# First expert, second half: seven block products, token sums on GpSimd, one scaling for both halves

## Chip, core and metric

One core of a Trainium2 chip runs the whole program in one launch. The metric is the device time of an execution in microseconds (us). The kernel before takes 1096.43 us (median of 3 runs, 1096.05 to 1096.6). The engines have one instruction queue each and run it in order: TensorE (PE in the profile; its weight loads are PEld), VectorE (DVE), ScalarE (ACT), GpSimd (POOL), SyncE (SP), which issues the DMAs here.

## The reference

```python
def _attn_ref(q, k, v, f):                  # (2, 8, 576, 64) each, f the forget gates
    scores = scale * q @ k.T + (cum[:, None] - cum[None, :])   # cum = cumsum(log f), causal
    return softmax(scores) @ v

def _moe_ref(x, w_gate, w1, w2):            # x: 1152 tokens x 512, 8 experts, 1024 hidden features
    P = np.exp(logits - logits.max())       # logits = x @ w_gate
    for _ in range(8):
        P /= P.sum(1, keepdims=True) + 1e-09
        P /= P.sum(0, keepdims=True) + 1e-09
        P *= N / E
    for e in range(E):
        h = np.maximum(x @ w1[e], 0.0)
        out += P[:, e:e + 1] * (h @ w2[e])
    return out

def _moe2_ref(x, w_in, w_out):              # 512 -> 2048 -> 512
    h = x @ w_in
    return (h * np.tanh(softplus(h))) @ w_out
```

Three layers one behind the other: attention, eight experts that all see every token with a weight P per token and expert, and a last feed-forward layer. The change lies at the start of the experts.

## The kernel before, in words

Every fp32 value that goes through TensorE is held as two parts, high and low ("h" and "l": ScalarE writes the high part as a rounded copy, VectorE or GpSimd the low part as the remainder, value minus high part). A product of two such values is three matmuls: high by high, high by low, low by high.

An expert's 1024 hidden features are two halves of 512; halves are numbered 0 to 15 over the eight experts. Tokens go in three chunks of 384 (`CH`). One plain unit (`l1`, line 816 on) is one feature block of 128 for one chunk: 4 input blocks by 3 matmuls of 384 columns, into one PSUM bank. `relu_split` (L832, L833) makes the two hidden parts from it. The second layer (`l2_tile`, L855) multiplies hidden blocks of 128 tokens by w2, 512 columns wide, three matmuls for each feature block.

From half 2 on the first layer isn't plain. `pair(half, n, tasks)` computes two feature blocks by two by a Strassen-like scheme with 7 block products in place of 8. It needs sums of blocks of w1 (S1 to S4: `new_sum`, `s_sum`, `s_split`) and sums of blocks of tokens (T1 to T3: `t_whole`, `t_diff`, `t_split`; `t_first` replaces one block of x by its sum with others). `t_whole` adds high and low parts back together, in two instructions of 576 columns; `t_diff` and `t_split` are 1152 columns wide. The tokens of a block fall in two sets of 288 columns, so there are two pairs for a half (n = 0 and 1), each with 14 products of 6 matmuls of 288 columns (`product`, L1263). Out of the PSUM banks ScalarE copies partial products ("snap", L1292), VectorE adds others to them ("c", L1297), and `relu_split` ends a block. The order within a pair is the list `plan`: products 1, 2, 1, 6, 2, 6, 7, 5, 7, 4, 5, 4, 3, 3 (each twice, for two feature blocks). `tasks` are small jobs that are put between these products: evictions, the splits of w2 (`w2_tasks`), pieces of a decoding of later weights.

The token sums serve all 15 later halves, as x doesn't change, so they are made once. In the kernel before this happens during the first expert, which is computed the plain way:

- Half 0, chunks 0 and 1, run as filler work between attention's steps, and are evicted to `acc[0..5]`.
- Then a loop over 8 feature blocks does chunk 2 of both halves: 8 plain units, and behind each the second layer of the one before, all into the three banks `psa`. Between them the background work goes: the splits of half 1's w1 and w2 (`bg`), the token sums (`tbg`, on VectorE), and the steps of the balancing iteration for P (`sinkhorn`, one part at each `step_side`; its column sums are small matmuls against a matrix `ones`).
- Then 8 plain units for half 1, chunks 0 and 1, with the rest of `tbg`, and `scale_first` for chunk 2 (ScalarE scales `psa` by P into `acc[6..8]`).
- Then `second(1, c)` for c = 0 and 1: the second layer of half 1, with the splits of half 2 and the scaling of `acc[0..5]` between. Its evictions add P times the bank to `acc`.

`second` takes `slots`, a list of jobs, one entry after each nine matmuls. Loads of weights are DMAs on SyncE (`Weights.load`, L61), each issued as soon as the buffer that it fills is split. The tile framework sets all waits; the order of instructions on each engine is the order of the code.

Of the kernel before, what the change touches and what calls it, by code (L numbers as in the profile page):

```python
# [83 lines left out]
def attention_moe_kernel(  # L84
# [734 lines left out]
    def l1(half, ft_, c, pool, tag="h"):  # L819
        w = wts.slots[half]  # L820
        fs = slice(ft_ * 128, (ft_ + 1) * 128)
        ph = pool.tile([128, 512], F32, tag=tag, name="ph")[:, :CH]
        for kk in range(KD):
            for n, (wn, x) in enumerate((("w1h", xh), ("w1h", xl), ("w1l", xh))):
                nc.tensor.matmul(  # L825
                    out=ph, lhsT=w[wn][kk][:, fs], rhs=x[c][:, kk],
                    start=(kk == 0 and n == 0), stop=(kk == KD - 1 and n == 2),
                )
        return ph
# [30 lines left out]
    def sinkhorn():  # L860
# [9 lines left out]
        nc.tensor.matmul(out=mb[:, :1], lhsT=ones[:1, :], rhs=m2, start=True, stop=True)  # L870
# [3 lines left out]
        for it in range(ITERS):  # L874
# [9 lines left out]
            nc.tensor.matmul(out=cp, lhsT=ones, rhs=cs, start=True, stop=True)  # L884
# [6 lines left out]
            )  # L891

# [156 lines left out]
    def new_sum(half, i, in0, in1, op):  # L1049
        t = sum_pool[0].tile([128, 2, 256], F32, tag="tmp", name="sum")  # L1050
        nc.vector.tensor_tensor(out=t, in0=in0, in1=in1, op=op)
# [12 lines left out]
    def s_split(half, i):  # L1064
# [3 lines left out]
        nc.vector.tensor_tensor(out=lo, in0=t, in1=f(hi), op=ALU.subtract)  # L1068
# [31 lines left out]
    hctx = ExitStack()  # L1100
    actx = ExitStack()
    hp = actx.enter_context(tc.tile_pool(name="hp", bufs=2))
    ttmp = actx.enter_context(tc.tile_pool(name="ttmp", bufs=1))
    ones = ttmp.tile([128, 128], F32, name="ones")
    nc.gpsimd.memset(ones, 1.0)
    ps_h = hctx.enter_context(tc.tile_pool(name="ps_h", bufs=2, space=PSUM))
    ps_a = hctx.enter_context(tc.tile_pool(name="ps_a", bufs=3, space=PSUM))

    def new_h():
        return (  # L1110
            hp.tile([128, CH], FR, tag="hh", name="hh"),
            hp.tile([128, CH], FR, tag="hlo", name="hlo"),
        )

    wts.load(1, 2, stage_b)

    def plain_split(n):
        wts.split(1, n // 2, n % 2)
        if n == 3:
            for p in (0, 1):  # L1120
                wts.raw.pop((1, p))
                wts.load(2, p, stage)

    bg = [lambda n=n: plain_split(n) for n in range(4)] + w2_tasks(1)


# [14 lines left out]
    def t_whole(r, side, k):  # L1141
        for n in range(2):
            nc.vector.tensor_tensor(
# [7 lines left out]
    def t_split(i, r):  # L1151
        hi, lo = (t[:, TW * (i - 1):TW * i] for t in (th, tl))
        nc.scalar.copy(out=hi, in_=r)
        nc.vector.tensor_tensor(out=lo, in0=r, in1=f(hi), op=ALU.subtract)

    def t_first(n):
# [3 lines left out]
        nc.vector.tensor_tensor(out=lo, in0=r, in1=f(hi), op=ALU.subtract)  # L1160

    tbg = [
        lambda: t_whole(r11, 0, 0),
        lambda: t_whole(r12, 1, 0),
        lambda: t_diff(r11, r12, r11),
        lambda: t_whole(r22, 1, 2),
        lambda: t_diff(r12, r22, r12),
        lambda: t_split(2, r12),
        lambda: t_diff(r22, r22, r11),
        lambda: t_split(1, r22),  # L1170
        lambda: t_whole(r12, 0, 2),
        lambda: t_diff(r12, r12, r22),
        lambda: t_split(3, r12),
    ]
# [3 lines left out]
    NF = F // 128
    step_side()
    for g in range(NF):  # L1180
        half, gg = g // 4, g % 4
        ph = l1(half, gg, 2, ps_h)
        h = new_h()
        relu_split(ph, *h)
        step_side()
        for _ in range(2):
            if bg:
                bg.pop(0)()
        for _ in range((0, 0, 0, 0, 1, 2, 2, 2)[g]):
            tbg.pop(0)()  # L1190
# [4 lines left out]
    firsts = [lambda j=j: scale_first(6 + j, psa[j]) for j in range(3)]
    firsts += [lambda t=t: scale_first(t, acc[t]) for t in range(6)]
    for g in range(4):
        for c in range(2):
            last_l1 = (g, c) == (3, 1)
            relu_split(l1(1, g, c, *((ps_m, "m") if last_l1 else (ps_h, "h"))), *hidden(g, c))  # L1200
            if g == 0 and c == 0:
                for j in range(3):
                    l2_tile(*prev[:2], psa[j], j, prev[2], prev[3] == 0, prev[3] == NF - 1)
            if side:
                if (g, c) != (0, 1):
                    step_side()
            elif len(firsts) > 6:
                firsts.pop(0)()
            if tbg and g:
                tbg.pop(0)()  # L1210
    assert not (bg or tbg or side)
    assert len(firsts) <= 6
    for n in range(2):
        t_first(n)
    actx.close()
    hctx.close()


    dec = mctx.enter_context(tc.tile_pool(name="dec", bufs=2))
    tmp = mctx.enter_context(tc.tile_pool(name="tmp", bufs=4))  # L1220
    sum_pool.append(tmp)
    ps_b = ctx.enter_context(tc.tile_pool(name="ps_b", bufs=1, space=PSUM))
    banks = [ps_b.tile([128, 512], F32, name=f"bank{i}") for i in range(7)]

    def next_bank():
        banks.append(banks.pop(0))
# [655 lines left out]
```

## Time and profile before

| | |
|---|---|
| median of 3 runs | 1096.43 us (1096.05 to 1096.6) |
| the profiled execution | 1096.1 us, span 1094.3 us |
| TensorE busy, of the span | 1085.1 us, 99% |
| VectorE | 842.0 us, 77% |
| ScalarE | 542.6 us, 50% |
| GpSimd | 75.5 us, 7%, none of it after 157.7 us |
| granted TensorE clock | 1.000 |
| chain that ended last | TensorE 91%, VectorE 4%, DMA 2%, ScalarE 1% |

The span is from the first to the last instruction; the execution's own time has 1.8 us more around it. Busy matmul times overlap each other, as a matmul starts before the one ahead of it has ended; the pace is read from the start times. The experts begin at 162.65 us, and the second expert's first product starts at 231.93.

### The profile page before, as it was taken

How to read it: one execution, taken by the hardware profiler on the slowest of the kernel's cores; microseconds unless marked ns; L12 is line 12 of the kernel's file. 1: busy time of each engine (PE TensorE's matmuls, PEld its weight loads, DVE VectorE, ACT ScalarE, POOL GpSimd, SP SyncE). 2: the span in 40 equal slices, each digit the busy share in tenths (PEclk: the TensorE clock that was granted, in tenths of full speed). 3: DMA queues.
4: the chain of work that ended last, by engine and by line, in shares of the span. 5: the costliest groups of instructions: out<-in, count | busy, mean ns of one | idle time of the engine just before them, and what ended most of it. 6: DMA issues, size and time to landing. Idle time of an engine off the chain costs nothing.

```text
span 1094.3 us, 18378 instructions
## 1 busy us (share of the span) xinstructions
PE 1085.1 (99%) x6838; PEld 964.9 (88%) x6838; DVE 842.0 (77%) x1891; ACT 542.6 (50%) x1287; POOL 75.5 (7%) x124
## 2 busy tenths in 40 slices
PE   9999999999999999999999999999999999999998
PEld 8787779998989899898888989899898989888997
DVE  7856647878787887977888796887877559778994
ACT  7756532444426243342624435252442448877872
POOL 6644410000000000000000000000000000000000
PEclk9999999999999999999999999999999999999999
DMA  6534202023242424425343342534323341261402
GB/s 147 147 84 113 65 21 78 1 97 124 87 137 68 144 86 146 136 78 155 97 153 96 118 150 92 154 87 145 116 89 95 115 156 48 68 202 51 172 1 87
DMA packets 103805, 114.98 MB, mean 105 GB/s; under 512 B 35236, under 2 KB 63860, under 8 KB 103716
## 3 DMA queue, kind: packets, MB, share of 16 engines
q1 hardware_dynamic: 103716, 113.81, 33.8%
q8 instruction: 54, 0.88, 0.3%
q14 instruction: 35, 0.29, 0.1%
HBM read 82.24 MB, written 27.07 MB: 100 GB/s over the span
## 4 chain that ended last, share of the span: by engine, by line
PE 91%; DVE 4%; DMA 2%; ACT 1%; issue 1%; SPq 0%; POOL 0%; DVEq 0%; ACTq 0%
PE bank L855 31%; PE bank L1263 27%; PE bank L1735 9%; PE bank L1645 4%; PE ph L825 3%; PE x L567 2%; PE spare L1645 2%; PE bank L1574 2%; PE pa L855 2%; PE pa L640 2%; PE ph L621 1%; DMA w_in_b<-hb 1%; PE sp L467 1%; PE pt L531 1%; PE pt L360 1%; PE sp L415 1%
## 5 line engine op out<-in xcount | busy, mean ns | idle before, releaser
L855 PE MATMUL bank<-w2h,big 128*128 128x512 f32 x924 | 300.2, 394 | 0.0
L855 PEld LDWEIGHTS bank<-w2h,big 128*128 128x128 f32 x924 | 173.8, 188 | 38.7 <-DVE hid_b L833 0.2
L855 PE MATMUL bank<-w2l,big 128*128 128x512 f32 x528 | 207.5, 393 | 0.0
L1292 ACT COPY snap<-bank 128x288 f32<-128x288 f32 x168 | 66.9, 398 | 170.3 <-PE bank L1263 169.9
L832 ACT ACTIVATE big<-c 128x288 fp32r<-128x288 f32 x168 | 75.2, 447 | 86.6 <-DVE c L1297 82.6
L855 PEld LDWEIGHTS bank<-w2l,big 128*128 128x128 f32 x528 | 99.3, 188 | 20.9
L833 DVE SCALAR_TENSOR_TENSOR big<-c,big 128x288 fp32r<-128x288 f32 x140 | 64.1, 458 | 57.1 <-ACT big L832 54.5
L1028 DVE SCALAR_TENSOR_TENSOR acc<-bank,P,acc 128x512 f32<-128x512 f32 x132 | 92.5, 747 | 19.3 <-PE bank L855 19.3
L1263 PE MATMUL bank<-tt,ss 128*128 128x288 f32 x672 | 103.5, 295 | 0.4 <-ACT snap L1292 0.4
L1263 PE MATMUL bank<-xh,ss 128*128 128x288 f32 x448 | 103.4, 296 | 0.2 <-DVE c L1297 0.2
L1263 PEld LDWEIGHTS bank<-tt,ss 128*128 128x128 f32 x672 | 93.9, 188 | 0.8 <-ACT snap L1292 0.8
L1297 DVE TENSOR_TENSOR c<-bank,snap 128x288 f32<-128x288 f32 x168 | 76.0, 453 | 19.7 <-PE bank L1263 19.4
L1263 PEld LDWEIGHTS bank<-xh,ss 128*128 128x128 f32 x448 | 76.7, 188 | 0.4 <-DVE c L1297 0.4
L1008 ACT CAST hb<-da 128x512 fp32r<-128x512 f32 x38 | 23.7, 623 | 107.3 <-DVE da L986 95.9
L1263 PE MATMUL bank<-xl,ss 128*128 128x288 f32 x224 | 66.5, 297 | 0.0
L1263 PE MATMUL bank<-xh,w1l 128*128 128x288 f32 x224 | 66.2, 295 | 0.0
L1263 PE MATMUL bank<-xl,w1h 128*128 128x288 f32 x224 | 66.1, 295 | 0.0
L1263 PE MATMUL bank<-xh,w1h 128*128 128x288 f32 x224 | 66.1, 295 | 0.0
L75 DVE TENSOR_TENSOR w2l<-stg,w2h 128x512 fp32r<-128x512 f32 x60 | 41.3, 690 | 14.0 <-ACT w2h L74 13.7
L855 PE MATMUL bank<-w2h,hid_b 128*128 128x512 f32 x132 | 51.6, 391 | 0.0
L511 POOL TENSOR_SCALAR p<-p,rs 128x256 f32<-128x256 f32 (+5 forms) x72 | 42.3, 598 | 65.1 <-DVE rs L507 42.9
L1263 PE MATMUL bank<-tt,w1h 128*128 128x288 f32 x224 | 46.4, 295 | 0.0
(314 smaller groups left out, 2460.7 us busy)
## 6 DMA issues: line engine op xcount, KB each, us to landing
stg<-in_moe_w_dram SPq DMA_DIRECT2D x64, 512.0 KB
wb<-w_in_b SPq DMA_DIRECT2D x42, 256.0 KB
raw<-in_moe_w_in_dram SPq DMA_DIRECT2D x16, 512.0 KB
raw<-in_moe_w_out_dram SPq DMA_DIRECT2D x16, 512.0 KB
w_in_b<-hb SPq DMA_DIRECT2D x18, 256.0 KB
w_out_h<-hb SPq DMA_DIRECT2D x16, 256.0 KB
w_out_l<-da SPq DMA_DIRECT2D x16, 256.0 KB
w_in_f<-da SPq DMA_DIRECT2D x12, 256.0 KB
```

What stands on the lines that cost most here:

```text
L75: (lo_engine or nc.vector).tensor_tensor(out=lo, in0=raw, in1=f(hi), op=ALU.subtract)
L511: nc.gpsimd.tensor_scalar(out=p[:n, a, :nk], in0=p[:n, a, :nk], scalar1=r[:n, a:a + 1], scalar2=1.0, op0=ALU.mult, op1=ALU.mult,)
L825: nc.tensor.matmul(out=ph, lhsT=w[wn][kk][:, fs], rhs=x[c][:, kk], start=(kk == 0 and n == 0), stop=(kk == KD - 1 and n == 2),)
L832: nc.scalar.activation(out=hh, in_=ph, func=AF.Relu)
L833: nc.vector.scalar_tensor_tensor(out=hl, in0=ph, scalar=0.0, in1=f(hh), op0=ALU.max, op1=ALU.subtract)
L855: nc.tensor.matmul(out=pa, lhsT=a_[:, ts_], rhs=w[wn][ft_], start=(first and n == 0), stop=(last and n == 2),)
L1028: nc.vector.scalar_tensor_tensor(out=acc[t], in0=pa, scalar=P[:, t, e:e + 1], in1=acc[t], op0=ALU.mult, op1=ALU.add)
L1263: nc.tensor.matmul(out=by_chunk(out_) if len(v_.shape) == 3 else out_, lhsT=u, rhs=v_, start=first and m == 0, stop=m == 5, skip_group_che ...
L1292: nc.scalar.copy(out=t, in_=bank["x", g])
L1297: nc.vector.tensor_tensor(out=t, in0=bank[of, g], in1=snap[with_, g], op=ALU.add)
L1645: nc.tensor.matmul(out=out_, lhsT=a_(kk, pa), rhs=b_(kk, pb), start=first and q == 0, stop=q == 5, skip_group_check=True,)
L1735: nc.tensor.matmul(out=bk[b][:, cs], lhsT=a_[:, ts_], rhs=w[wn][i][:, cs], start=i == 0 and q == 0, stop=i == 3 and q == 2,)
```

## The change

Half 1 goes through `pair` like the halves behind it. What the plain units hid before has to be ready sooner: the loop at the start shrinks to the four units of half 0, chunk 2, and the sums of w1's blocks for half 1 are needed too. So work moves to GpSimd: `t_whole`, the sums of w1's blocks, most of the low parts of half 1's weights and sums, and the low parts of T3 and of one half of `t_first`. Expert 0's halves are added without P (`evict` for e = 0 is an addition; `settle` copies `psa` to `acc[6..8]`), and all nine parts are scaled during the second expert. The scratch pool `tmp` and the seven PSUM banks are opened ahead of the loop; the decoding's first transfers come behind the first pair. `ones` is replaced by a broadcast column, and `sinkhorn` stops twice in an iteration instead of once.

```diff
@@ sinkhorn
-            nc.tensor.matmul(out=cp, lhsT=ones, rhs=cs, start=True, stop=True)
+            nc.tensor.matmul(out=cp, lhsT=one_row.to_broadcast([128, 128]), rhs=cs, start=True, stop=True)
...
+            yield
@@ evict
         t = c * 3 + j
+        if e == 0:
+            nc.vector.tensor_tensor(out=acc[t], in0=pa, in1=acc[t], op=ALU.add)
+            return
@@ new_sum
-        nc.vector.tensor_tensor(out=t, in0=in0, in1=in1, op=op)
+        (nc.vector if half > 1 else nc.gpsimd).tensor_tensor(out=t, in0=in0, in1=in1, op=op)
@@ s_split
-        nc.vector.tensor_tensor(out=lo, in0=t, in1=f(hi), op=ALU.subtract)
+        (nc.vector if half > 1 or i == 2 else nc.gpsimd).tensor_tensor(out=lo, in0=t, in1=f(hi), op=ALU.subtract)
@@ t_whole
-            nc.vector.tensor_tensor(
+            nc.gpsimd.tensor_tensor(
@@ t_split
-        nc.vector.tensor_tensor(out=lo, in0=r, in1=f(hi), op=ALU.subtract)
+        (nc.gpsimd if i == 3 else nc.vector).tensor_tensor(out=lo, in0=r, in1=f(hi), op=ALU.subtract)
@@ t_first
-        nc.vector.tensor_tensor(out=lo, in0=r, in1=f(hi), op=ALU.subtract)
+        (nc.gpsimd if n else nc.vector).tensor_tensor(out=lo, in0=r, in1=f(hi), op=ALU.subtract)
@@ the loop at the start (the loops over 8 blocks and over half 1's chunks 0 and 1, bg and tbg are removed)
+    nxt = w1_tasks(1, nc.gpsimd)
+    work = [
+        [nxt[0], nxt[1], lambda: t_diff(r11, r12, r11)],
+        [lambda: t_diff(r12, r22, r12), nxt[2], lambda: t_diff(r22, r22, r11)],
+        [lambda: t_split(2, r12), nxt[4], lambda: t_whole(r12, 0, 2), nxt[3]],
+        [lambda: t_split(1, r22), nxt[5], lambda: t_diff(r12, r12, r22)],
     ]
+    step_side()
+    t_whole(r11, 0, 0)
+    t_whole(r12, 1, 0)
+    t_whole(r22, 1, 2)
+    psa = banks[2:5]
+    units_in = [banks[0], banks[1]]
...
+    def l2_first(g, h):
+        for j in range(3):
+            l2_tile(0, g, psa[j], j, h, g == 0, g == 3)
+
+    for g in range(4):
+        ph = l1(0, g, 2, units_in[g % 2])
...
         relu_split(ph, *h)
+        if g in (0, 2):
+            step_side()
+        for t in work[g]:
+            t()
         if prev:
+            l2_first(*prev)
+        prev = (g, h)
+    l2_first(*prev)
+    t_split(3, r12)
+    banks = [banks[i] for i in (5, 6, 0, 1, 2, 3, 4)]
+    def settle(j):
+        (nc.scalar.copy if j in (2,) else nc.vector.tensor_copy)(out=acc[6 + j], in_=psa[j])
+
+    firsts = [lambda t=t: scale_first(t, acc[t]) for t in range(NT)]
@@ the loop over halves
+        w2t = w2_tasks(half, nc.gpsimd if half == 1 else None)
+        if half == 1:
+            pair(1, 0, {1: [nxt[6]], 2: [lambda: t_first(0)], 3: [lambda: settle(0)], 4: [lambda: settle(1)], 5: [lambda: settle(2)], 6: [w2t[0]], 7: [nxt[7]], 9: [lambda: t_first(1), actx.close], 10: [w2t[1], step_side]})
+            dec = mctx.enter_context(tc.tile_pool(name="dec", bufs=2))
+            fetch()
+            fetch()
+            pair(1, 1, {1: [step_side], 3: [w2t[2]], 5: [step_side], 6: [w2t[3]], 10: [step_side]})
+        else:
...
-            slots = [[nxt[0]], [nxt[1]], [nxt[2]], [nxt[3]], [], [nxt[4], nxt[5]], [nxt[6], one], [nxt[7]]]
-            slots[0] += firsts[:3]
-            slots[2] += firsts[3:]
+            slots = [
+                [nxt[0]], [nxt[1], step_side], [nxt[2], step_side], [nxt[3], step_side],
+                [step_side], [nxt[4], step_side], [nxt[5], step_side], [nxt[6], step_side],
+                [step_side], [nxt[7], step_side], [step_side], [step_side, one],
+            ]
+        if half == 2:
+            step_side()
+            assert not side
+            for n in range(3):
+                slots[n] += firsts[3 * n:3 * n + 3]
         evicts = []
-        for c in range(NCH if half > 1 else 2):
+        for c in range(NCH):
```

## Rows read from the trace of the kernel before

**Rows 1.** The page: busy time and share of an engine; the chain that ended last.
```profile
PE 1085.1 (99%) x6838; PEld 964.9 (88%) x6838; DVE 842.0 (77%) x1891; ACT 542.6 (50%) x1287; POOL 75.5 (7%) x124
...
PE 91%; DVE 4%; DMA 2%; ACT 1%; issue 1%; SPq 0%; POOL 0%; DVEq 0%; ACTq 0%
```

**Rows 2.** Windows: length, busy us (instructions) of each engine, clock, DMA.
```profile
162.60:231.90 69.30, 69.30 (x356) 62.63 (x356) 54.45 (x127) 26.45 (x47) 0.00 (x0) 1.00 0.18 61
...
256.50:281.00 24.50, 24.50 (x114) 20.34 (x113) 21.97 (x39) 5.92 (x12) 0.00 (x0) 1.00 0.45 151
```

**Rows 3.** Timeline, TensorE: start, duration, line, out<-in, count; first and last of each width.
```profile
205.33 0.34 PE L825 MATMUL ph<-xh,w1h 128*128 128x384 f32 x1
...
207.42 0.34 PE L825 MATMUL ph<-xh,w1h 128*128 128x384 f32 x1
...
216.36 0.39 PE L855 MATMUL bank<-w2l,big 128*128 128x512 f32 x1
...
220.48 0.39 PE L855 MATMUL bank<-w2l,big 128*128 128x512 f32 x1
...
231.93 0.29 PE L1263 MATMUL bank<-xh,w1h 128*128 128x288 f32 x1
...
234.32 0.96 PE L1263 MATMUL bank<-tt,ss 128*128 128x288 f32 x6
```

**Rows 4.** Timeline, TensorE: the small matmuls that follow the third unit.
```profile
171.63 0.28 PE L884 MATMUL cp<-cs,ones 128*128 128x8 f32 x2
```

**Rows 5.** GpSimd's lines by shape, whole run: count, busy us, mean ns, idle before.
```profile
L320 POOL TENSOR_TENSOR hl<-raw,hl 128x512 fp32r<-128x512 f32 x10 | 12.8, 1281 | 5.9 <-PE sp L468 4.9 <-ACT hl L316 0.4 <-POOL qb L282 0.4
...
L773 POOL TENSOR_TENSOR wgc<-wg,wgc 128x32 fp32r<-128x32 f32 x1 | 0.3, 253 | 0.1
```

**Rows 6.** Timeline, GpSimd: subtractions in attention, and its last instruction.
```profile
40.27 1.39 POOL L320 TENSOR_TENSOR hl<-raw,hl 64x512 fp32r<-64x512 f32 x1 [0.46 <-DVE hl L318]
...
43.76 1.27 POOL L320 TENSOR_TENSOR hl<-raw,hl 64x512 fp32r<-64x512 f32 x1
...
57.54 1.65 POOL L320 TENSOR_TENSOR hl<-raw,hl 64x512 fp32r<-64x512 f32 x1 [2.68 <-DVE hl L318]
...
60.68 1.28 POOL L320 TENSOR_TENSOR hl<-raw,hl 128x512 fp32r<-128x512 f32 x1
...
157.45 0.21 POOL L1105 MEMSET ones<- 128x128 f32 x1 [6.57 <-PE x L567]
```

**Rows 7.** Timeline, VectorE: what it did at the same times.
```profile
40.55 1.65 DVE L328 TENSOR_TENSOR big<-stg,big 128x512 fp32r<-128x512 f32 x1
...
44.46 1.11 DVE L328 TENSOR_TENSOR big<-stg,big 128x512 fp32r<-128x512 f32 x1 [0.45 <-ACT big L324]
...
57.37 0.68 DVE L328 TENSOR_TENSOR big<-stg,big 128x512 fp32r<-128x512 f32 x1
...
61.87 0.56 DVE L629 SCALAR_TENSOR_TENSOR xl<-ph,xh 128x384 fp32r<-128x384 f32 x1 [0.35 <-ACT xh L628]
```

**Rows 8.** VectorE's lines by shape, 162.6 to 231.9; one row of its timeline.
```profile
L1149 DVE TENSOR_TENSOR r<-r,r 128x1152 f32<-128x1152 f32 x4 | 5.4, 1354 | 0.1
L75 DVE TENSOR_TENSOR w1l<-stg,w1h 128x512 fp32r<-128x512 f32 x8 | 5.3, 682 | 0.0
...
L879 DVE TENSOR_TENSOR P<-P,r 128x72 f32<-128x72 f32 x8 | 1.9, 234 | 0.3
...
174.78 1.28 DVE L75 TENSOR_TENSOR w2l<-stg,w2h 128x512 fp32r<-128x512 f32 x2
```

**Rows 9.** Timeline, ScalarE: a wait for a load, a high part, a scaling, a snap.
```profile
180.00 1.14 ACT L74 CAST w2h<-stg 128x512 fp32r<-128x512 f32 x2 [3.19 <-DMA stg<-in_moe_w_dram]
...
205.17 1.15 ACT L1153 CAST tt<-r 128x1152 fp32r<-128x1152 f32 x1
...
207.49 0.69 ACT L1040 ACTIVATE acc<-pa,P 128x512 f32<-128x512 f32 x1
...
232.97 0.40 ACT L1292 COPY snap<-bank 128x288 f32<-128x288 f32 x1 [6.13 <-PE bank L1263]
```

More of the change, by code (lines that the diff above doesn't have):

```diff
@@ L817, in attention_moe_kernel, with l1 @@
     ps_m = ctx.enter_context(tc.tile_pool(name="ps_m", bufs=1, space=PSUM))
-    def l1(half, ft_, c, pool, tag="h"):
+    def l1(half, ft_, c, pool):
         w = wts.slots[half]
         fs = slice(ft_ * 128, (ft_ + 1) * 128)
-        ph = pool.tile([128, 512], F32, tag=tag, name="ph")[:, :CH]
+        ph = pool[:, :CH]
         for kk in range(KD):
@@ L869, in sinkhorn @@
         mb = ps_m.tile([128, 8], F32, tag="m", name="mb")
-        nc.tensor.matmul(out=mb[:, :1], lhsT=ones[:1, :], rhs=m2, start=True, stop=True)
+        nc.tensor.matmul(out=mb[:, :1], lhsT=one_row[:1].to_broadcast([1, 128]), rhs=m2, start=True, stop=True)
         nm = small.tile([128, 1], F32, tag="nm", name="nm", bufs=1)
@@ L1097, in w2_tasks, with next_bank @@
         return [lambda n=n: task(n) for n in range(4)]
-    hctx = ExitStack()
+    tmp = mctx.enter_context(tc.tile_pool(name="tmp", bufs=4))
+    sum_pool.append(tmp)
+    banks = []
+    for i, n in enumerate((2, 3, 2)):
+        ps_b = ctx.enter_context(tc.tile_pool(name=f"ps_b{i}", bufs=1, space=PSUM))
+        banks += [ps_b.tile([128, 512], F32, name=f"bank{len(banks) + j}") for j in range(n)]
+    def next_bank():
+        banks.append(banks.pop(0))
+        return banks[-1]
     actx = ExitStack()
-    hp = actx.enter_context(tc.tile_pool(name="hp", bufs=2))
     ttmp = actx.enter_context(tc.tile_pool(name="ttmp", bufs=1))
[L1104 to L1113, printed above, removed]
-    wts.load(1, 2, stage_b)
[L1117 to L1124, printed above, removed]
+    wts.load(1, 2, stage_b)
     r11, r12, r22 = (ttmp.tile([128, TW], F32, name=f"r{n}") for n in (11, 12, 22))
@@ L1159, in t_first @@
         nc.scalar.copy(out=hi, in_=r)
-        nc.vector.tensor_tensor(out=lo, in0=r, in1=f(hi), op=ALU.subtract)
[L1162 to L1173, printed above, removed]
-    ]
@@ L1176, in attention_moe_kernel @@
-    psa = [ps_a.tile([128, DM], F32, tag="a", name="pa") for _ in range(3)]
-    prev = None
[L1178 to L1183, printed above, removed]
-        relu_split(ph, *h)
[L1185 to L1190, printed above, removed]
-        if prev:
-            for j in range(3):
-                l2_tile(*prev[:2], psa[j], j, prev[2], prev[3] == 0, prev[3] == NF - 1)
-        prev = (half, gg, h, g)
@@ L1195, in attention_moe_kernel @@
[L1195 to L1226, printed above, removed]
-        return banks[-1]
+        (nc.gpsimd if n else nc.vector).tensor_tensor(out=lo, in0=r, in1=f(hi), op=ALU.subtract)
@@ new lines, in l2_first @@
+    def l2_first(g, h):
[3 more added lines that the diff above has]
+        ph = l1(0, g, 2, units_in[g % 2])
+        o = 2 * TW + CH * (g % 2)
+        h = (hid_b[:, o - 2 * TW:o - 2 * TW + CH], tl[:, o:o + CH])
+        relu_split(ph, *h)
+        if g in (0, 2):
+            step_side()
+        for t in work[g]:
+            t()
+        if prev:
+            l2_first(*prev)
+        prev = (g, h)
+    l2_first(*prev)
+    t_split(3, r12)
@@ L1349, in attention_moe_kernel @@
     last_half = 2 * E - 1
-    fetch()
-    fetch()
     evicts = []
@@ L1355, in attention_moe_kernel @@
         one, two, three = (lambda n=n: piece(n) for n in (1, 2, 3))
-        if half > 1:
-            w2t = w2_tasks(half)
+        w2t = w2_tasks(half, nc.gpsimd if half == 1 else None)
[6 more added lines that the diff above has]
+        else:
             evicts[0]()
```

## The prediction

> **What bounds the kernel now.** I read the engines' busy times and the chain that ended last first [rows 1]: TensorE is busy in 99% of the span and makes 91% of the chain, so a microsecond counts only if it is TensorE's. Then the table by stretch [rows 2]. The change lies between the end of attention and the second expert, 162.6 to 231.9 us. TensorE is busy in all of it (69.30 of 69.30) at full clock, VectorE in 54.45, ScalarE in 26.45, GpSimd in nothing. So now everything that feeds TensorE is in time, and any new wait costs what it lasts. The profiled run took 1096.1 us (span 1094.3 and 1.8 around it); the median shown, 1096.43, is 0.3 above. I add to the run and put the 0.3 on at the end.
>
> **TensorE's own work.** Its pace comes from start times [rows 3]: a 384-column matmul every 2.09/12 = 0.174 us, a 512-column one every 4.12/18 = 0.229, a 288-column one every 2.39/18 = 0.133. The second half of expert 0 loses 12 units of 12 matmuls of 384 columns (three chunks by four feature blocks): 144 x 0.174 = 25.1. It gains two pairs of 14 products of 6 matmuls of 288: 168 x 0.133 = 22.3. Its 144 second-layer matmuls of 512 and the small column-sum matmuls stay. Gain: 2.8 us, and no more than that is to be had.
>
> **What must be ready, and when.** Before, 8 further plain units and their second layer gave the helpers time; now only four units of half 0 stand between attention and the products, which need all sums of tokens and weights. Up to the third unit the order on TensorE is unchanged; the trace has its end at 171.63 [rows 4]. From there: three groups of nine 512-column matmuls (6.2), the fourth unit (2.1), three products of 0.80, three changeovers of 0.1: TensorE arrives at the fourth product, number 6, at about 182.6. That one needs the bank that ScalarE empties (first "snap"), and in ScalarE's queue this stands behind the high part of T3. T3 is a difference on VectorE of a token sum that GpSimd forms last, after eight 512-wide weight sums and remainders.
>
> **GpSimd's price.** A subtraction of 512 columns takes it 1.281 us, one of 32 columns 0.253 [rows 5], so 2.14 ns a column and, my estimate, 1.42 for half a token sum (576). It is free at 157.45, where it clears "ones" now [rows 6]. Eight half sums and eight of 512 alone: 157.45 + 11.4 + 10.2 = 179.1. With the difference 1.35 [rows 8], the high part 1.15, the snap 0.40 [rows 9] and 0.3 of handovers the fourth product could start at 182.3. That would just fit.
>
> **The gate between GpSimd and VectorE.** It does not fit, because the two don't run side by side on such work. In attention, where GpSimd subtracts too, I laid their timelines over each other. GpSimd works from 40.27 to 41.66; the VectorE subtraction issued at 40.55, 0.68 elsewhere [rows 8], takes 1.65 and ends at 42.20. The pair at 43.76 and 44.46 does the same. The other way round, a VectorE subtraction from 57.37 to 58.05 makes the GpSimd one issued at 57.54 last 1.65, against 1.28 [rows 6, 7]. The VectorE instruction at 61.87 has the same neighbour (60.68 to 61.96) and keeps its 0.56: it reads one operand from PSUM. So two instructions that read all operands from SBUF go one after the other: a waiting VectorE one ends 0.54 behind GpSimd (per 512 columns; 1.22 for 1152), a waiting GpSimd one 1.13 behind VectorE.
>
> Now the queue. GpSimd's first six half sums meet nobody: 157.45 + 6 x 1.42 = 166.0. From then to the end of the last token sum the gate passes eight GpSimd instructions of 512 (8 x 1.13 = 9.0), two of 576 (2 x 1.27 = 2.5) and five of VectorE's of 1152: three differences, two remainders (5 x 1.22 = 6.1). That is 17.6: 183.6. The next weight remainder of GpSimd is queued already and goes first (1.13), then VectorE's last difference (1.22), T3's high part (1.15), the snap (0.40), handovers 0.3: 187.8. Behind the waiting difference VectorE holds the first pair's additions, behind the high part ScalarE holds every snap, and TensorE waits for both. Stall: 187.8 - 182.6 = 5.2, wherever in this stretch it shows (some of it may show before the last 512-column group, whose relu remainder stands behind a waiting token remainder on VectorE).
>
> Three shorter ones follow in the first pair, TensorE running on from 187.8. Product 7 at 190.2 needs the third weight remainder, which VectorE can only do when GpSimd's 1152-wide remainder (2.65, from 187.5) is over: 0.5. Product 5 needs a bank that VectorE copies out after that remainder, a relu remainder and a token remainder: 0.9. Product 3 needs GpSimd's fourth weight remainder behind a remainder of w2: 0.6. Column sums and the second pair: 0.2. Together 2.2, between 0 (all hidden in the first stall) and 3.5.
>
> This rests on 512-wide instructions. The expert-balance steps on VectorE also have products of 72 columns from SBUF (0.234 each, [rows 8]), and no row shows these beside GpSimd's subtractions. The Trainium skill, "SBUF — State Buffer", section "Who interferes with whom", goes further than the rows: any VectorE instruction with two SBUF inputs waits for a whole GpSimd instruction that reads SBUF. By it two more waits of up to 1.1 us come ahead of the token remainders, and the sum would be some 0.8 higher; by the rows alone it stays as it is.
>
> **The other parts.** Expert 0 is summed unscaled: nine additions in place of six multiply-adds and three more copies on VectorE and ScalarE; the copies are counted above. The nine scalings (0.69 each, [rows 9]) move into the second expert's first three steps of nine matmuls, where ScalarE is busy 5.92 of 24.5 us now [rows 2]: 2.07 more in each step of 2.07, so it is late by what else it has there, some 3 us; the evictions that read the result come a step later than the fourth, 8 us on. Nothing. Loads of the next w1 are issued when GpSimd's fourth remainder is done, about 180 instead of 171; they are needed where half 1's second layer begins, twelve steps of 2.07 before the end of the stretch, about 211. The second half of w2 is loaded behind a GpSimd remainder at about 200; such a load came 3.9 us after its release (174.78 + 1.28 to 180.00, [rows 8, 9]), so at 204, when ScalarE asks for it: 0, at most 1. The broadcast vector of ones costs nothing; the first decode transfers now go behind the first pair, 20 us ahead of use.
>
> **Sum.** -2.8 + 5.2 + 2.2 = +4.6: 1100.7, with the 0.3 about 1101.0.
>
> **Rivals.**
> (a) The two engines do run side by side here, or the gate is cheap. For it: the schedule without it fits to 0.3 us; against it: every row of such a pair. Then no stall but 0.3 at product 3: -2.5, 1093.9. It decides from the point where GpSimd's last token sum ends before about 179.5. Chance 0.17.
> (b) The gate is there but half of it is covered: GpSimd gets ahead while VectorE waits for ScalarE, or its first sum starts when the attention's last transposes are done, three us before 157.45. Stall 2.5 to 4 in all: -0.3 to +1.2, about 1097. For it: VectorE is idle 15 us of the stretch. Against it: the last token sum overwrites a buffer that VectorE's remainder must have read, so an early start helps little. Chance 0.20.
> (c) GpSimd is slower on the token blocks (strides never shown on it), or keeps the gate from one ready instruction to the next: 10% on its 21.6 us of sums and some 8 us of remainders behind them makes 3.0 more, 1104.0. Chance 0.10.
> (d) The forecast, 1098.6 to 1103.5: 0.53.
>
> About 0.2% (2.2 us) is what a measurement of this kernel tells from no change. (c) and (d) are slower: 0.63. (b) is within it: 0.20. (a) is just beyond it: 0.17. The range runs from (a) to (c), 1094.0 to 1104.5.
>
> **What would show it.** Right: in the new profile TensorE waits some 5 us in all before the first product 6 for ScalarE's snap or the relu remainder ahead of it, and VectorE's 1152-column differences last 1.9 to 2.5 us instead of 1.35 wherever GpSimd is at work. Step by step: matmul pace 0.174, 0.229, 0.133; GpSimd 1.28 for 512 columns and 1.42 for 576; the last token sum ends near 183.6. Wrong: VectorE's differences keep 1.35 beside GpSimd, or GpSimd's last token sum ends by 180.

## The result, and the profile after

The changed kernel takes 1105.84 us (median of 5 runs, 1105.46 to 1105.98); the kernel before took 1096.07 in the same session (5 runs). The ratio is 1.0086, 95% interval 1.0075 to 1.0097: slower by 9.8 us, where 4.6 were forecast. The direction was right, the size was not, and the time lies above the range. Single executions can come out some 5 us longer at a lower mean clock (the kernel before, in another session: 1095.98 at 1.000, 1101.48 at 0.993), so medians are compared.

| | before | after |
|---|---|---|
| span of the profiled run | 1094.3 | 1103.7 |
| first product of half 2 (the second expert's first) starts | 231.93 | 240.70 |
| first product of half 3 starts ("the next pair" below) | 279.17 | 288.03 |
| TensorE above its pace, 162.6 to the first product of half 2 | 1.6 | 13.2 |

The last row adds up, over all matmuls of the stretch, how much later the next one starts than the paces of [rows 3] say. Halves 2 and 3 begin 8.8 and 8.9 us late, and behind that the kernels run in step: nearly all of the loss lies before 240.7.

The page after: busy time by engine, and the chain that ended last (before: [rows 1]). GpSimd now has 112.8 us, and VectorE's share of the chain has grown, with a line of its own for the token differences (L1140, 1%).

```profile
PE 1085.9 (98%) x6862; PEld 963.6 (87%) x6862; DVE 850.1 (77%) x1895; ACT 548.5 (50%) x1308; POOL 112.8 (10%) x148
...
PE 88%; DVE 6%; ACT 2%; DMA 1%; issue 1%; POOL 1%; SPq 0%; DVEq 0%; ACTq 0%; POOLq 0%
```

The stretch of [rows 2], and three windows in it (length, then busy us of TensorE, its weight loads, VectorE, ScalarE and GpSimd; then the granted clock).

```profile
162.60:240.70 78.10, 69.47 (x380) 61.02 (x379) 60.97 (x125) 28.03 (x59) 32.61 (x22) 0.98 0.17 54
171.85:176.29 4.44, 0.40 (x2) 0.00 (x0) 4.44 (x3) 0.00 (x0) 2.71 (x3) 1.00 0.35 118
176.29:179.75 3.46, 3.46 (x8) 2.81 (x9) 3.10 (x4) 0.29 (x2) 0.00 (x0) 0.51 0.00 0
188.13:191.52 3.39, 0.30 (x3) 0.06 (x1) 1.87 (x2) 1.50 (x3) 3.25 (x3) 1.00 0.01 2
```

TensorE stands still twice, 4.2 and 3.3 us beyond one matmul's pace. Between the two it runs 3.46 us at a granted clock of 0.51, the lower of its two levels (1.2 of 2.4 GHz): eight matmuls there cost 1.7 us more than at the pace of [rows 3]. What TensorE's queue waited for in the stretch (total, times, longest):

```profile
PEld bank L855 <- DVE tt L833: 4.5, 1, 4.5
PEld bank L1225 <- ACT snap L1254: 3.9, 2, 3.3
PEld bank L1225 <- DVE acc L1188: 1.1, 1, 1.1
PEld bank L1225 <- POOL ss L1072: 0.5, 1, 0.5
```

The first is unit 1's ReLU remainder, the second the snapshot ahead of the first product 6: the two places that the prediction named. Why the first is late stands on VectorE's timeline (start, duration):

```profile
165.96 0.27 DVE L867 TENSOR_REDUCE m<-mt 1x1 f32<-1x128 f32 x1
166.16 9.62 DVE L1140 TENSOR_TENSOR r<-r,r 128x1152 f32<-128x1152 f32 x1
175.69 0.54 DVE L833 SCALAR_TENSOR_TENSOR tt<-bank,hid_b 128x384 fp32r<-128x384 f32 x1
176.16 1.34 DVE L1140 TENSOR_TENSOR r<-r,r 128x1152 f32<-128x1152 f32 x1
...
187.57 2.41 DVE L1140 TENSOR_TENSOR r<-r,r 128x1152 f32<-128x1152 f32 x1 [2.73 <-POOL r L1134]
```

The first token difference lasts 9.62 us, 1.35 alone [rows 8], and the ReLU remainder behind it starts at 175.69. GpSimd's timeline over the same time:

```profile
157.46 8.44 POOL L1134 TENSOR_TENSOR r<-xh,xl 128x576 f32<-128x576 f32 x6 [6.60 <-PE x L567]
165.84 1.31 POOL L1055 TENSOR_TENSOR sum<-stg 128x512 f32<-128x512 f32 x1
167.09 1.30 POOL L75 TENSOR_TENSOR w1l<-stg,w1h 128x512 fp32r<-128x512 f32 x1
...
173.28 1.28 POOL L1055 TENSOR_TENSOR sum<-stg,sum 128x512 f32<-128x512 f32 x1
181.46 2.10 POOL L75 TENSOR_TENSOR w1l<-stg,w1h 128x512 fp32r<-128x512 f32 x1 [6.91 <-ACT w1h L74]
183.54 4.00 POOL L1134 TENSOR_TENSOR r<-xh,xl 128x576 f32<-128x576 f32 x2
187.50 3.62 POOL L1072 TENSOR_TENSOR ss<-sum,ss 128x512 fp32r<-128x512 f32 x2
```

Seven instructions of 512 run back to back from 165.84 to 174.56, none longer than 1.31. The difference ends at 175.78, which is 1.22 behind the seventh: it had the gate only when GpSimd ran dry (its eighth waits until 181.46 for ScalarE, whose work hangs on VectorE). At 187.57 it is otherwise: the last difference asks during one of the two at 187.50, ends 1.22 behind it, and the second of the two waits.

### The profile page after: what moved, and what is told of

It reads as the page before. It is cut to its first block, busy times and chain, and to the rows that moved or that the text cites. A ratio compares the mean times of both kernels' runs of the same rounds, so it can differ in the third digit from the quotient of the medians.

```text
span 1103.7 us, 18491 instructions
## 1 busy us (share of the span) xinstructions
PE 1085.9 (98%) x6862; PEld 963.6 (87%) x6862; DVE 850.1 (77%) x1895; ACT 548.5 (50%) x1308; POOL 112.8 (10%) x148
## 4 chain that ended last, share of the span: by engine, by line
PE 88%; DVE 6%; ACT 2%; DMA 1%; issue 1%; POOL 1%; SPq 0%; DVEq 0%; ACTq 0%; POOLq 0%
PE bank L855 32%; PE bank L1225 28%; PE bank L1708 9%; PE bank L1618 4%; PE x L567 2%; PE spare L1618 2%; PE bank L1547 2%; PE pa L640 2%; PE ph L621 1%; DVE r L1140 1%; DMA w_in_b<-hb 1%; PE sp L467 1%; PE pt L360 1%; PE pt L531 1%; PE sp L415 1%
## 5 line engine op out<-in xcount | busy, mean ns | idle before, releaser
L855 PE MATMUL bank<-w2h,big 128*128 128x512 f32 x945 | 307.8, 394 | 0.0
L832 ACT ACTIVATE big<-c 128x288 fp32r<-128x288 f32 x180 | 80.2, 446 | 95.1 <-DVE c L1259 91.0
L833 DVE SCALAR_TENSOR_TENSOR big<-c,big 128x288 fp32r<-128x288 f32 x150 | 69.2, 461 | 60.6 <-ACT big L832 57.7
L1225 PE MATMUL bank<-tt,ss 128*128 128x288 f32 x720 | 111.7, 296 | 4.1 <-ACT snap L1254 4.0
L1225 PE MATMUL bank<-xh,ss 128*128 128x288 f32 x480 | 111.0, 296 | 1.2 <-DVE acc L1188 0.8
L1225 PEld LDWEIGHTS bank<-tt,ss 128*128 128x128 f32 x720 | 100.6, 188 | 5.5 <-ACT snap L1254 5.1
L1259 DVE TENSOR_TENSOR c<-bank,snap 128x288 f32<-128x288 f32 x180 | 81.2, 451 | 19.8 <-PE bank L1225 17.7
L1225 PEld LDWEIGHTS bank<-xh,ss 128*128 128x128 f32 x480 | 82.2, 188 | 2.0 <-DVE acc L1188 1.1
L1225 PE MATMUL bank<-xh,w1h 128*128 128x288 f32 x240 | 70.9, 296 | 0.0
L1225 PE MATMUL bank<-xl,w1h 128*128 128x288 f32 x240 | 70.9, 295 | 0.0
```

The source lines that it names most:

```text
L832: nc.scalar.activation(out=hh, in_=ph, func=AF.Relu)
L833: nc.vector.scalar_tensor_tensor(out=hl, in0=ph, scalar=0.0, in1=f(hh), op0=ALU.max, op1=ALU.subtract)
L855: nc.tensor.matmul(out=pa, lhsT=a_[:, ts_], rhs=w[wn][ft_], start=(first and n == 0), stop=(last and n == 2),)
L1225: nc.tensor.matmul(out=by_chunk(out_) if len(v_.shape) == 3 else out_, lhsT=u, rhs=v_, start=first and m == 0, stop=m == 5, skip_group_che ...
L1259: nc.vector.tensor_tensor(out=t, in0=bank[of, g], in1=snap[with_, g], op=ALU.add)
```

## The experiments

Theory 1, made from these rows: GpSimd keeps the gate as long as it has a ready instruction. Theory 2, the prediction's: the gate alternates, and the 9.62 us have another reason. The same-session time of the kernel before is given with each ratio.

**The gate by itself (e1_gate).** Rows of ready GpSimd subtractions against VectorE instructions that start in their midst.

```diff
+for i in range(n):                      # n = 1, 2, 3, 4, 8
+    nc.gpsimd.tensor_tensor(out=g[i], in0=a, in1=b, op=ALU.subtract)
+nc.scalar.copy(out=s, in_=t)            # VectorE starts about 0.6 us in
+nc.vector.tensor_tensor(out=c[0], in0=s, in1=b, op=ALU.subtract)
```

> This kernel computes nothing of the reference: GpSimd does rows of 1, 2, 3, 4 and 8 ready subtractions of 512 columns (1.28 us each in the changed kernel), and VectorE one of 512 (0.69 alone) that starts some 0.6 us into the row; then rows of 8 against VectorE instructions of 1152, 72 columns, a copy, one that reads PSUM, and six in a row. Theory 1, GpSimd keeps the gate from one ready instruction to the next: VectorE's lasts until the row's end, about 1.3, 2.6, 3.9, 5.2 and 10.3 us for 1, 2, 3, 4 and 8, and GpSimd's stay at 1.28. Theory 2, the gate alternates as the prediction has it, and the 9.62 us in the changed kernel have another reason: 1.2 to 1.9 us whatever the row's length, and one of GpSimd's instructions is longer by some 0.6. The one that reads PSUM lasts about 0.6 by both. Six in a row: theory 1, the first takes all of the wait and the other five 0.69; theory 2, each waits for about one of GpSimd's.

VectorE's timeline: one against a row of eight, one that reads PSUM, one of 72 columns, six in a row.

```profile
32.45 1.22 DVE L53 TENSOR_TENSOR c<-s,b 128x512 f32<-128x512 f32 x1 [0.74 <-ACT s L44]
...
71.41 0.69 DVE L57 TENSOR_TENSOR c<-pt,s 128x512 f32<-128x512 f32 x1 [0.74 <-ACT s L44]
...
81.59 0.76 DVE L53 TENSOR_TENSOR c<-s,b 128x72 f32<-128x72 f32 x1 [0.74 <-ACT s L44]
...
102.14 9.55 DVE L53 TENSOR_TENSOR c<-s,b 128x512 f32<-128x512 f32 x6 [0.74 <-ACT s L44]
```

GpSimd's seven beside those six:

```profile
102.77 11.27 POOL L34 TENSOR_TENSOR g<-a,b 128x512 f32<-128x512 f32 x7
```

1.21 to 1.22 us whatever the row's length, and the six take turns with GpSimd's (9.55 for six). Theory 2 holds here, theory 1 doesn't. PSUM as one source is free of the gate; 72 columns are not. A copy of 512 from SBUF to SBUF waits too: it takes 0.95 and ends 0.29 behind GpSimd's instruction.

**VectorE's order (e2_order).** 1105.56, ratio 1.0079 (1.0056 to 1.0103) to 1096.29.

```diff
-[nxt[0], nxt[1], lambda: t_diff(r11, r12, r11)],
-[lambda: t_diff(r12, r22, r12), nxt[2], ...
+[nxt[0], nxt[1]],
+[lambda: t_diff(r11, r12, r11), lambda: t_diff(r12, r22, r12), nxt[2], ...
```

> Only VectorE's order is changed: the remainder behind unit 1's ReLU goes ahead of the first token difference. Theory 1 (GpSimd keeps the gate until it runs dry at about 174.6): the difference still ends at about 175.8 although it begins some 6 us later; the 4.2 us stop before unit 1's second tiles and the 1.7 us of half clock behind it go, but the later differences end no more than 0.6 us earlier, so that the stop before the first product 6 grows from 3.3 to about 8.5: total 1105.2, between 1104.2 and 1106. Rival: the two stops are separate prices, and the 5.9 us come back: about 1100. Theory 2 (no keeping; the difference was slow for where it began): it lasts 1.4 to 2.5 us, ends by about 174, and the total is 1102 to 1103.

VectorE's difference, and TensorE's waits of the stretch:

```profile
168.05 7.72 DVE L1140 TENSOR_TENSOR r<-r,r 128x1152 f32<-128x1152 f32 x1
```
```profile
PEld bank L1225 <- ACT snap L1254: 5.0, 2, 4.4
PEld bank L855 <- DVE tt L833: 3.5, 2, 3.2
PEld bank L855 <- ACT hid_b L832: 1.5, 1, 1.5
```

It begins 1.9 us later and ends at 175.8 as before. Unit 1's stop is gone, and 8.5 us of stops stand at units 2 and 3 and before product 6; behind the last of them the clock is 0.58 from 191.20 to 195.10. Where VectorE's queue is cut decides only where TensorE stops: the chain through the differences decides how long (the next pair starts at 288.04, in the changed kernel at 288.03).

**All on VectorE (e3_vector).** GpSimd keeps the six early half token sums. 1100.25, ratio 1.0035 (1.0018 to 1.0053) to 1096.29.

```diff
-(nc.vector if half > 1 else nc.gpsimd).tensor_tensor(out=t, ...        # sums
+nc.vector.tensor_tensor(out=t, ...
-(nc.vector if half > 1 or i == 2 else nc.gpsimd).tensor_tensor(out=lo, # sum remainders
+nc.vector.tensor_tensor(out=lo,
...
```

> GpSimd keeps only the six early half token sums (they end at 165.9); all its other work of this half goes to VectorE, about 12 us more there (4 weight sums, 4 + 4 weight remainders and 3 sum remainders of 0.69, 2 half token sums of 0.7, 1.35 and 0.7 for the token remainders; 4 x 0.69 of it behind product 6). Theory 1: no VectorE instruction lasts over 1.4 us from 166 on, the clock is 1.00 throughout, no wait is longer than 2 to 4 us; VectorE's first difference loses 8.3 us, and the added work ahead of the first product 6 gives back about 6: 1098.5 to 1102, faster than the changed kernel. Theory 2: GpSimd's help is worth more than the gate costs: 1106 to 1112.

```profile
162.60:200.00 37.40, 33.15 (x195) 29.60 (x194) 31.88 (x59) 17.97 (x37) 3.26 (x3) 1.00 0.16 54
```

The difference lasts 1.34, the clock of the profiled run is 1.00, the longest stop is 2.9 us (unit 3's ReLU remainder in VectorE's queue), and the next pair starts at 282.05. GpSimd's share from 166 on makes the changed kernel some 5.5 us slower than all on VectorE: the opposite of help.

**GpSimd waits for VectorE (e4_yield).** 1106.36, ratio 1.0084 (1.0053 to 1.0116) to 1096.29.

```diff
+def after(r): nc.gpsimd.tensor_copy(out=seen, in_=r[:, :1])
+[lambda: t_diff(r11, r12, r11), lambda: after(r11), nxt[0], nxt[1]],
+[lambda: t_diff(r12, r22, r12), lambda: t_diff(r22, r22, r11), lambda: after(r22), nxt[2]],
```

> The engines keep their work, but GpSimd waits (by a copy of one column) for the first difference before its first weight sum, and for the third difference before its third. Theory 1: the first difference lasts 1.4 to 2.0 us and the stop before unit 1's second tiles, with the half clock, is gone (5.9 us); GpSimd's next row of four (5.1 us) then holds the second difference until about 173, GpSimd ends its weight sums some 3 to 4 us later than now, and the stop before the first product 6 becomes 4 to 9 us: total 1101 to 1105. Theory 2 (alternation): the second difference waits for one instruction only (2 to 2.6 us) and ends by about 175; about 1101 as predicted for the changed kernel.

VectorE's second difference, then GpSimd's row beside it:

```profile
168.10 2.13 DVE L1140 TENSOR_TENSOR r<-r,r 128x1152 f32<-128x1152 f32 x1
```
```profile
167.73 1.29 POOL L1055 TENSOR_TENSOR sum<-stg 128x512 f32<-128x512 f32 x1
168.98 2.40 POOL L75 TENSOR_TENSOR w1l<-stg,w1h 128x512 fp32r<-128x512 f32 x1
171.34 2.41 POOL L1055 TENSOR_TENSOR sum<-sum,stg 128x512 f32<-128x512 f32 x1
```

Here the same instructions alternate: theory 1 falls as a rule. And next to nothing is won: GpSimd ends later, the stop before product 6 is 5.6 us, and behind it TensorE runs 5.8 us at half clock (2.7 us lost). The median lies above what either theory gave, but it stands between two groups: 1104.02 and 1104.27 (the profiled one), inside theory 1's answer, and 1108.44 and 1108.71, at mean clocks of 0.992 and 0.990.

**What decides who is next (e5_rows, e10_around).** Two more kernels of rows, with the changed kernel's shapes and strides, and with long rows, ScalarE, TensorE and loads beside them.

```diff
+six(); seven()        # the changed kernel's half token sums, sums, remainders
+ask(n, diff)          # VectorE's 1152 difference, n ScalarE copies later
```

> This kernel computes nothing of the reference: it asks why VectorE's 1152 difference waited over seven of GpSimd's instructions in the changed kernel (9.62 us) and over one alone in the rows of the first gate kernel. Seven stretches, in each one difference of 1152 (in place, 1.35 alone) against a row of GpSimd's: rows of 12 subtractions of 512, asked for in the third, the fifth or sixth and the eighth (1 to 3); the seven sums and remainders in the changed kernel's shapes (4); the six half token sums in its strides and then the seven, asked for in the first of the seven, as there (5); the six and seven plain ones (6); six plain ones of 576 and the seven (7). Theory A, the length of the row that GpSimd has behind it decides: 2 to 2.7 us in stretches 1 and 4, some 9 in 3, 5, 6 and 7. Theory B, the shapes decide: 9 to 10 in 4, 5 and 7, and 2 to 2.7 in 1, 2, 3 and 6. Theory C, the token sums' strides ahead of it: 9 to 10 in 5 and 6 alone. Theory D, something around it in the kernel: 1.4 to 2.7 in all seven.

> This kernel computes nothing of the reference. Open is what made GpSimd keep the gate over seven instructions in the changed kernel, when it gave way at the next boundary in every other place. Seven stretches, one 1152 difference of VectorE in each: rows of 20 plain instructions of GpSimd, asked for some 11 and 16 us into them (1, 2); the changed kernel's six and seven, asked for in the second and third of the seven (3, 4); the same with ScalarE's copies that the seven read made while the row runs (5), with TensorE at work (6), with loads landing in SBUF (7). If a long hold by GpSimd decides (8.7 and 10.6 us there, under 8.7 in all rows that gave way): 1 to 4 and 6, 7 wait for the row's end, 4 to 12 us. If what runs beside it decides: 5, 6 or 7 alone. If none of these: 1.4 to 2.7 us in all seven, and the reason stays open.

The one that copies the changed kernel most closely (e5_rows), and the longest of the second kernel, asked 0.06 us before the end of a GpSimd instruction while TensorE was at work:

```profile
88.76 2.34 DVE L59 TENSOR_TENSOR r<-r,r 128x1152 f32<-128x1152 f32 x1
```
```profile
139.01 2.52 DVE L61 TENSOR_TENSOR r<-r,r 128x1152 f32<-128x1152 f32 x1
```

1.35 to 2.52 in all fourteen stretches; two that asked 0.06 us or less before the end of an instruction had to let one more pass. So shapes, strides, a long hold and busy neighbours do not bring it about one by one, as far as these rows imitate the place.

**Asked for early, and half a wait (e7_early, e8_half).** e7: 1103.04, ratio 1.0049 (1.0030 to 1.0068) to 1096.30. e8: 1103.34, ratio 1.0058 (1.0037 to 1.0078).

```diff
-[nxt[0], nxt[1], lambda: t_diff(r11, r12, r11)],   # the changed kernel
+[nxt[0], nxt[1]],                                  # e7, and in the loop, ahead of unit 0's relu_split:
+if g == 0: t_diff(r11, r12, r11)
+[lambda: t_diff(r11, r12, r11), lambda: after(r11), nxt[0], nxt[1]],  # e8: as e4, without its second wait
```

> The changed kernel with VectorE's first token difference ahead of unit 0's ReLU remainder: it asks for the gate at about 163.7, inside GpSimd's fifth half token sum, with nine more ready instructions of GpSimd behind that one. If GpSimd gives way (as it did in every row of the two gate kernels): the difference lasts about 2.1 us, GpSimd's row ends 1.2 later, the stop before unit 1's second tiles and its half clock are gone, and the total is 1100 to 1103: this is then the price of the change with the gate alternating. If GpSimd keeps the gate until it runs dry: the difference lasts some 11 us, unit 0's remainder waits behind it, the stop stands before unit 0's second tiles and is longer (7 us): 1106 to 1110.

> Half of the kernel in which GpSimd waits: it waits for the first difference alone, before its first weight sum, and then has its row of seven ready, as in the changed kernel. If the gate alternates: the second and third difference last 2.1 to 2.4 us each, GpSimd's row of seven ends near 177.5 in place of 174.6, and without the second wait its later instructions are 1 to 2 us ahead of that kernel's: total 1102 to 1105, a stop of 3 to 5 us before the first product 6. If GpSimd keeps the gate whenever its row is ready: the second difference lasts about 8 us and the total is 1105 to 1108.

e7's first difference, what TensorE waited for, and the window behind its longest stop:

```profile
163.50 2.15 DVE L1140 TENSOR_TENSOR r<-r,r 128x1152 f32<-128x1152 f32 x1
```
```profile
PEld bank L1227 <- ACT snap L1256: 6.2, 2, 5.6
PEld bank L855 <- DVE tt L833: 0.4, 1, 0.4
PEld bank L1227 <- POOL ss L1072: 0.3, 1, 0.3
```
```profile
188.10:191.64 3.54, 3.52 (x15) 3.53 (x15) 3.48 (x4) 2.08 (x5) 2.38 (x1) 0.50 0.00 0
```

With an alternating gate the change costs 5.4 us up to the next pair (284.58 against 279.17): one stop of 5.6 before product 6, 1.6 us of half clock behind it, 0.9 of short stops, less what TensorE gains. e8, where GpSimd gives way too, starts the next pair at 285.71, with the same stop of 5.6 where 3 to 5 were expected. e8 also shows how small an instruction may be and still wait, VectorE's 9-wide and 72-wide steps of the normalisation (0.17 and 0.23 alone):

```profile
173.74 1.22 DVE L877 TENSOR_SCALAR r<-r 128x9 f32<-128x9 f32 x1
...
175.25 1.03 DVE L879 TENSOR_TENSOR P<-P,r 128x72 f32<-128x72 f32 x1
```

**A break in the row, and another instruction in front (e12_tiny, e13_ask).** 1106.47, ratio 1.0075 (1.0053 to 1.0096), and 1106.36, ratio 1.0074 (1.0049 to 1.0100), to 1097.10.

```diff
+nc.gpsimd.tensor_copy(out=seen[:, :1], in_=seen[:, 1:])   # e12: ahead of the seven
+nc.vector.tensor_tensor(out=seen[:, :32], ...)            # e13: ahead of t_diff(r11, ...)
```

> The changed kernel with one tiny GpSimd instruction more (a copy of one column that waits for nothing) between the six half token sums and the seven. In the kernel where GpSimd waited there for VectorE, it gave way in all of the seven. If a break in the row of large instructions is what lets VectorE in: the first difference lasts about 2.1 to 2.6 us, and the total is that of the kernel with the difference asked for early, 1102.5 to 1104. If it is that VectorE had used the gate just before: the difference still lasts some 9.6 us and the total stays at 1105 to 1106.5.

> The changed kernel with one small VectorE instruction more (32 columns, both operands from SBUF) right ahead of the first token difference, so that it asks for the gate in the place of the difference and the difference some 0.1 us after it has had it. If GpSimd keeps the gate against whatever asks at this place until its row runs dry: the small one lasts some 8.4 us, the difference begins near 174.6 as now, and the total is 1105 to 1106.5. If it keeps it against that instruction alone, or gives way once VectorE has had it within the row: the small one lasts 0.1 to 1.2 us, the difference 2 to 2.6, and the total is 1102.5 to 1104.5.

VectorE in e12, and in e13:

```profile
166.09 1.33 DVE L1140 TENSOR_TENSOR r<-r,r 128x1152 f32<-128x1152 f32 x1
...
168.04 9.36 DVE L1140 TENSOR_TENSOR r<-r,r 128x1152 f32<-128x1152 f32 x1
```
```profile
166.92 8.80 DVE L1157 TENSOR_TENSOR seen<-seen 128x32 f32<-128x32 f32 x1
```

In e12 the first difference gets in at once, by the tiny copy (which waits 1.42), and the second waits for the seven instead: half of each expectation, and no gain. In e13 even 32 columns wait 8.80. So it is neither that one instruction nor an unbroken row. What decides it stays open: with the same seven instructions GpSimd kept the gate in four kernels (after, e2, e12, e13) and gave way in three (e4, where a second wait splits the seven, e7, e8). Each kernel was profiled in one execution; whether another execution of the same kernel would do otherwise is not shown.

These two also bear on the clock. First e12's window behind a stop of 3.1 us at unit 2, then e13's behind one of 2.1 before product 6; the share of clock granted is the third figure from the end.

```profile
179.32:182.30 2.98, 2.98 (x7) 2.21 (x8) 2.42 (x8) 2.93 (x6) 0.94 (x1) 0.51 0.00 0
```
```profile
192.68:197.01 4.33, 4.33 (x21) 4.33 (x22) 4.27 (x5) 2.31 (x6) 2.39 (x1) 0.61 0.00 0
```

In the changed kernel TensorE ran at full clock behind its second stop, of 3.3 us.

**A mixture (e6_mixed, e9_later, e11_behind).** All reasons for the stops addressed at once: GpSimd keeps two weight sums, four remainders of 512 and one of 576; the third and fourth pairs of half token sums go to VectorE; each ReLU remainder stands ahead of long token work; the three settling copies are ScalarE's; normalisation steps come later. In the lists, W and D are half token sums and token differences, t the parts of a token sum, f a weight sum with the parts of a block of w1, p the parts of a weight sum, "side" a step of the normalisation; in `on_pool` s is a weight sum, l a low part of w1, x1 one half of `t_first`.

```diff
+on_pool = ('l1', 'l2', 'p0', 'p3', 's1', 's2', 'x1')
+before_relu = [["W22", "D11"], ["f2", "f0"], ["t2", "f1", "side"], ["t1"]]
+behind_relu = [["side"], ["D12", "D22"], ["p0"], ["f3", "p1", "p2"]]
 # e9: four decoding steps from half 7's second products into half 8's block products
+more = {n: [one] for n in (5, 7, 8, 11)} if half == 8 else {}
+if half == 7: slots[9:11] = [[nxt[7]], []]
 # e11: the second "side" and "p0" behind unit 2's remainder
+... ["t2", "f1"], ["t1"]]    ... ["side"], ["p0", "f3", "p1", "p2"]]
```

> A version with all three reasons for the stops addressed: the third pair of half token sums on VectorE in its idle time; of GpSimd's share only two weight sums, four remainders of 512 and one of 576; each ReLU remainder ahead of long token work in VectorE's queue; the three settling copies on ScalarE; three of the normalisation's steps later. If the stops are VectorE's queue and the gate's sum (my theory now), those of the kernel with all on VectorE (2.9 us at the last unit and 2.4 in the products) shrink to about 2 in all, with no half clock: 1094.5 to 1098. Rival: any GpSimd work on the gate there costs more than it saves, since it takes the gate for 1.28 us where VectorE takes 0.69: 1100 to 1104.

> The mixed version, with four steps of the decoding for the last stage moved some 6 us later, from the end of the seventh half's second products into the eighth's block products: there a ScalarE copy waited 4.8 us for a DMA to land (517.4) and the snapshot behind it stopped TensorE for 1.4 us (0.5 in the kernel before). If ScalarE's queue was the reason, the stop shrinks to 0.3 or less: 1094.7 to 1095.6, 0.1 to 0.2% faster than before. If the DMA's landing shifts with it, the stop moves to a later product and the total stays at 1096.3.

> The mixed version with its decoding later, and the normalisation's second step and the first sum's remainder behind unit 2's ReLU remainder: there VectorE's 72-wide product waited 1.1 us for GpSimd's remainder, and the step as a whole held the ReLU remainder back by 3.1 us, so that TensorE stopped for 1.5 us. If that order was the reason, the stop goes and at most 0.5 us of it comes back at unit 3: 1093.9 to 1094.8, faster than before by 0.1 to 0.2%. If VectorE is the bound through the whole stretch, the 1.5 us come back in the products: 1095 to 1095.6.

| | us | before | ratio | next pair starts | span |
|---|---|---|---|---|---|
| e6 | 1096.33 | 1096.78 | 0.9991 (0.9970 to 1.0012) | 278.44 | 1095.4 |
| e9 | 1095.27 | 1096.30 | 0.9992 (0.9980 to 1.0005) | 278.36 | 1093.3 |
| e11 | 1094.96 | 1096.52 | 0.9987 (0.9977 to 0.9998) | 278.14 | 1093.2 |

ScalarE in e6, where a copy waits for a transfer with two snapshots queued behind it; then e11's first window:

```profile
517.45 0.62 ACT L1009 CAST hb<-raw 128x512 fp32r<-128x512 f32 x1 [4.78 <-DMA w_in_b<-hb]
517.98 0.69 ACT L1279 COPY snap<-bank 128x288 f32<-128x288 f32 x2
```
```profile
162.60:200.00 37.40, 36.18 (x225) 33.48 (x224) 34.75 (x63) 21.43 (x45) 11.98 (x8) 1.00 0.20 66
```

e6 starts the next pair 0.7 us ahead of the kernel before, but its span is 1.1 longer: 1.6 us more stop at 515 to 530, behind that copy. This execution of e6, 1097.14, is the longest of those at full clock (1095.48 to 1097.14), so the others need not all have that stop. e9's profile is without it and keeps the 0.8, though its interval still holds 1. e11 loses unit 2's stop and finds 1.2 us of it again in the products: its time lies between the two answers. It is the one version that is faster than both kernels, by 0.13%, just outside its uncertainty. VectorE is busy 34.75 of the 37.40 there, so little room is left on it. No run has the mixture's order with all work on VectorE, so what GpSimd's remaining share is worth is not shown.

## Why the prediction was wrong

**TensorE's gain, 2.8 us: right.** 13.2 - 1.6 = 11.6 us of new stops and slow matmuls, and the next pair is 8.9 late: 2.7 to 2.8 came in. e11, with 1.75 us of new stops, is ahead by the other 1.0.

**When TensorE would reach product 6, 182.6: right.** It stopped there at 188.26; less the 4.2 of the first stop and the 1.7 of slow clock that is 182.4.

**GpSimd's durations: right.** 1.45 for 576 columns (1.42 said), 1.27 to 1.31 for 512.

**The gate: its existence right, its turns wrong. This is the step that failed.** The prediction had "a waiting VectorE one ends 0.54 behind GpSimd (per 512 columns; 1.22 for 1152)" and let the two take turns, so that the last token sum ends at 183.6. The 1.22 was exact, but behind the seventh GpSimd instruction, not the first. Everything after it moved: the last token sum ended at 187.54. The first stall, 5.2 in the sum, was 7.5 (4.2 at unit 1, 3.3 at product 6). Of the signs to look for, one of four differences lasted what was said (2.41), two met nobody (1.34 and 1.36), one took 9.62. The kernels in which GpSimd gives way show about what this step cost: the next pair starts at 284.58 in e7 and at 285.71 in e8 in place of 288.03, 3.4 and 2.3 us sooner. Both also move the order of work a little, so this is no exact price. Rival (c) named this behaviour ("keeps the gate from one ready instruction to the next") at 3.0 more and a chance of 0.10. Why GpSimd kept the gate here and gave way elsewhere stays open.

**A term that was missing: the clock.** The prediction took every matmul at full pace. Behind a stop of 4.2 us the granted clock was 0.51 for 3.46 us, 1.7 us lost; in e7 behind 5.6 us 1.6 lost. Even where GpSimd gave way this term was there. With it and the gate alternating, the forecast of +4.6 would have been 6.2 up to the next pair, where e7 measured 5.4.

**The shorter stops: 2.2 said, 2.7 measured** (0.36 at product 7, 1.1 at product 5, 0.5 at product 3, 0.7 in the second pair, 0.1 behind the first stall). Right in place and nearly in size.

**The other parts: nothing, as said,** with 0.6 of waiting for the second load of w2 that ScalarE had and TensorE did not feel. Behind the stretch 0.5 more was lost in the span; a third of a microsecond of it is stops around 525 (1.36 against 1.03), of the kind that e9 removes.

The sum against the forecast: first stall +2.3, clock +1.7, shorter stops +0.5, behind the stretch +0.5, together 5.0 of the 5.2 missed; the median lies 0.4 above the profiled run. **The 72-wide products:** they met no GpSimd instruction in the changed kernel (0.23), but wherever they do in e4, e7 and e8 they wait, as a 9-wide TENSOR_SCALAR does. The Trainium skill, "SBUF — State Buffer", section "Who interferes with whom", names both kinds: two SBUF inputs contend with a GpSimd instruction that reads SBUF, and `tensor_scalar` can. The runs agree (1.03 and 1.22).

## What to carry to other kernels

Where VectorE is full, moving its all-SBUF work to GpSimd was no relief here: each such instruction takes the gate for 1.28 us where VectorE needs 0.69, and a VectorE instruction with two SBUF inputs stands still meanwhile. What costs VectorE nothing is GpSimd's work while VectorE reads PSUM or waits, and turns at the gate are not to be relied on. In a stage that TensorE fills, price a stop of some 4 us at its length and the half clock behind it (1.4 to 2.8 us lost here), and look for the in-order queue (a copy that waits for a transfer) that will swallow the gain further on.

## What the runs showed of the hardware

- The one that waits at the gate is usually next, but not always: 9.62, 7.72, 9.36 and 8.80 us in four kernels, until GpSimd ran dry. In all other places a difference of 1152 took 1.33 (alone) to 2.52. Why is open.
- Every stop of 4.2 us or more had the lower clock behind it, for 2.9 to 5.8 us (1.4 to 2.8 us lost). Shorter ones went both ways: full clock behind 2.9 (e2, e3) and 3.3 us (the changed kernel), the lower one behind 3.1 (e12) and, from 0.9 us after its end on, behind 2.1 (e13).
- In a row of turns, VectorE's subtraction of 512 takes 1.74 with its wait and GpSimd's 1.70: the two together are as slow as one after the other.
